# Linear attention followed by a noisy top-2 mixture of experts: queries turned and loaded ahead of keys, key decay on POOL, masks on SyncE's queue

## The chip, the cores and the metric

The kernel runs on one core of a Trainium2 chip. The core has five engines that run side by side and wait for each other through semaphores: TensorE (PE in the profile; its weight loads are PEld), VectorE (DVE), ScalarE (ACT), GpSimd (POOL) and SyncE (SP, which here only issues DMAs). The metric is device microseconds of one execution.

## The reference

Attention with decay over 4 batches, 8 heads, 768 positions and 64 channels, in blocks of 64, and then a mixture of 8 experts on its 3072 rows, each row going to its two best experts.

```
rel = pos[:, None] - pos[None, :]
Dmask = where(rel >= 0, lam ** rel, 0)            # one per head
lam_pow = lam ** (pos + 1);  rev_pow = lam ** (block - 1 - pos)
for b in range(nb):
    intra = (qb @ kb.T * Dmask) @ vb
    inter = (qb * lam_pow) @ kv_state
    out[:, :, sl] = intra + inter
    kv_state = lam ** block * kv_state + (kb * rev_pow).T @ vb
x = out, one row of 512 per token
noisy = x @ w_gate + log1p(exp(x @ w_noise)) * noise
top2 of noisy, weights by softmax of the two
out[token] = sum over its two experts e of weight * (relu(x @ w1[e]) @ w2[e])
```

## The kernel before

**Stages.** The attention works on blocks of 128 positions, two at a time: NST = 12 stages of 256 positions, three to a batch (w = u % 3). Loop number t of the main loop (line 956) finishes stage t and prepares stage u = t + 1. On PE it issues, in this order: the gate products of stage t - 1 (`products`), the turning of its output (`turn_x`), the transposes of keys and queries of stage u (`trans_k`, `trans_q`), the products of keys and values for the state (`kv`), the two halves of the output of stage t (`intra`, `inter`), the logits, and the scores of stage u (`scores`). Each engine takes its instructions strictly in the order in which this program issues them.

**Buffers in PSUM.** `bank()` gives out four buffers named pS in turn. A stage takes eleven: two for `turn_x`, two for the first of the two transposes, two for the other, one for `kv`, four for `scores`. So each waits until the one that was given out four places earlier has been read: the buffer of `kv` is the one that held the first half of the transposes issued first (before: the keys, copied out by four ACT copies on line 331).

**Who reads what.** The transposed keys go to SBUF by ACT in eight copies of 64 partitions (kT), the transposed queries by ACT in two (qT). DVE multiplies the same query buffer with the query scales QS (qTs, line 349), masks the scores (at, line 375) and does the routing work, which the loop hands out in small pieces through `advance(...)`: between the parts of `kv`, behind the logits, and 18 to 24 pieces behind the masking. These pieces exist from t = 4 on. POOL multiplies the states, issues the stores of x and the scattered writes of token lists (lst), and splits weights into high and low parts from t = 5 on (w1l, w2l, line 794).

**Key decay.** `kdecay(u)` (line 351) multiplies keys by the decay factors into KD, which `kv(u)` reads. KD has one buffer. POOL does stages 0 and 1, DVE the ten others.

**Start.** A table of powers of lam is built on DVE, turned by PE, written to DRAM (powd, issued on ACT's queue) and read back twice into the mask tile mrev, named at in the profile, since it takes a buffer of at (lines 227 to 229, ACT's queue). `make_mask` copies it to Mk. QS is a product of four matmuls (line 225) with hsel, which lies in KD's buffer, and pw. SyncE's queue loads lam, then kt, qt, vt of stage 0, then those of stage 1. `keep_warm` issues idle bf16 matmuls.

**Tail.** Behind the loop (lines 1011 to 1019) come the last gate products and logits, the transposes of the first two tiles of expert 0 (`trans_rows`), and its first matmuls. From there the experts run one after the other, from line 1037 on.

Of the kernel before, what the change touches and what calls it, by code (L numbers as in the profile page):

```python
# [21 lines left out]
FT = mybir.dt.float32  # L22
# [4 lines left out]
AF = mybir.ActivationFunctionType  # L27
# [3 lines left out]
B, H, S, D = 4, 8, 768, 64  # L31
C = 128
NC = S // C
NCH = B * NC
HP = H // 2
# [19 lines left out]
NST = NCH // 2  # L55
# [8 lines left out]
ZEROS = {11: 8}  # L64
MID = 16
X1 = ((), (), (), (), (0, 1), (2, 3, 4), (5, 6))
WARM = (10, 1, 1)
GB = (0, 8, 16, NCH)
NG = len(GB) - 1
GM = max(GB[i + 1] - GB[i] for i in range(NG))  # L70
# [17 lines left out]
def sub(ap, offset, dims):  # L88
    return bass.AP(tensor=ap.tensor, offset=ap.offset + offset, ap=dims)
# [27 lines left out]
def kernel(  # L117
# [3 lines left out]
    nc = tc.nc  # L121
# [4 lines left out]
    psum = ctx.enter_context(tc.tile_pool(name="psum", bufs=1, space=bass.MemoryType.PSUM))  # L126
# [9 lines left out]
    powd = dram.tile([256, H], FT, name="powd")  # L136
# [5 lines left out]
    QT, KT, VT = {}, {}, {}  # L142

    def load(u, nm):

        if u >= NST:
            return
        b, w = divmod(u, NW)
        at = b * H * S * D + w * 2 * C * D
        store, src, n = {"qt": (QT, q, 2), "kt": (KT, k, 2), "vt": (VT, v, 3)}[nm]  # L150
        if nm == "qt":
            store[u] = aw.tile([128, 2, H, D], FT, name=nm, bufs=n)
            for a in range(2):
                nc.sync.dma_start(store[u][:, a], sub(src, at + a * C * D, [[D, 128], [S * D, H], [1, D]]))
            return
        store[u] = aw.tile([128, H, 2, D], FT, name=nm, bufs=n)
        step = H if u else H // 2
        for h in range(0, H, step):
            nc.sync.dma_start(store[u][:, h:h + step].rearrange("p h e d -> p h (e d)"),
                              sub(src, at + h * S * D, [[2 * D, 128], [S * D, step], [1, 2 * D]]))  # L160
# [24 lines left out]
    hsel = aw.tile([128, H, 2, D], FT, name="kd", bufs=1).rearrange("p h e d -> p (h e d)")[:H, :HP * C]  # L185
    hsel = hsel.rearrange("h (p s i) -> h p s i", s=2, i=64)
    nc.vector.tensor_copy(hsel, identf[:H, :H].rearrange("h (p s) -> h p s", s=2)[:, :, :, None].to_broadcast([H, HP, 2, 64]))
    pp2 = aw.tile([128, 2 * DB * C], FT, name="xo", bufs=1)[:H, :512].rearrange("p (a i) -> p a i", a=2)
    pw = pp2[:, 0, :]
    nc.vector.memset(pw[:, 128:129], 1.0)  # L190
    nc.vector.tensor_copy(pw[:, 127:128], lamc)
    for i in range(7):
        n = 1 << i
# [5 lines left out]
    p = psum.tile([128, 3, H], FT, name="pL")  # L199
# [5 lines left out]
    mrev = aw.tile([128, C, H], FT, name="at")  # L205
    load(0, "vt")
    Mk = [ac.tile([128, HP, 1 + C], FT, name=f"Mk{s}") for s in range(2)]
    kdc = ac.tile([128, H, 2], FT, name="kdc")
# [11 lines left out]
        return sub(m, 2 * r * (1 + C), [m.ap[0], [1 + C, 2], [1, 2], [1, C]])  # L220

    QS = ac.tile([128, HP, C], FT, name="QS")
    p = psum.tile([128, HP, C], FT, name="pL")
    for hp in range(HP):
        nc.tensor.matmul(p[:, hp, :], hsel[:, hp].rearrange("h s i -> h (s i)"), pw[:, 127::-1], start=True, stop=True)
    nc.scalar.activation(QS, p, AF.Copy)
    for a in range(2):
        nc.scalar.dma_start(mrev[a * 64:(a + 1) * 64].rearrange("p i h -> p (i h)"),
                            sub(powd, 0, [[2 * H, 64], [1, C * H]]))

    for nm in ("kt", "qt", "vt"):
        load(1, nm)
# [87 lines left out]
    def trans_k(u):  # L320

        kT[u] = [aw.tile([128, HP, C], FT, name=f"kT{x}", bufs=1) for x in range(2)]
        for r in range(2):
            p = bank()
            for h in range(4):
                nc.tensor.transpose(p[:, h, :], KT[u][:, 4 * r + h].rearrange("p e d -> p (e d)"), identf)
            for x in range(2):
                for s in range(2):
                    out, src = kT[u][x][half(s), 2 * r:2 * r + 2, :], p[half(s ^ x), s::2, :]
                    if u or x:  # L330
                        nc.scalar.activation(out, src, AF.Copy)  # L331
                    else:
                        nc.vector.tensor_copy(out, src)

    def trans_q(u, scaled=True):

        qT[u] = aw.tile([128, HP, 2 * C], FT, name="qT", bufs=1)
        qTs[u] = aw.tile([128, HP, 2 * C], FT, name="qTs")
        for a in range(2):
            p = bank()  # L340
            for hp in range(HP):
                nc.tensor.transpose(p[:, hp, :], QT[u][:, a, 2 * hp:2 * hp + 2, :], identf)
            cs = slice(a * C, (a + 1) * C)
            if u:
                nc.scalar.activation(qT[u][:, :, cs], p, AF.Copy)
            else:
                nc.vector.tensor_copy(qT[u][:, :, cs], p)
            if scaled and (u % NW or a):
                nc.vector.tensor_mul(qTs[u][:, :, cs], p, QS)

    def kdecay(u):
        if u >= NST:
            return
        KD[u] = aw.tile([128, H, 2, D], FT, name="kd", bufs=1)
        n, eng = (H // 2, nc.gpsimd) if u < 2 else (H, nc.vector)
        for h in range(0, H, n):
            eng.tensor_mul(KD[u][:, h:h + n], KT[u][:, h:h + n], kdc[:, h:h + n, :, None].to_broadcast([128, n, 2, D]))

    TURNS = ((0, 0), (1, 1), (0, 1), (1, 0))

# [69 lines left out]
    def products(u):  # L430

        p = psum.tile([128, 2, C], FT, name="pR")
        for d in range(DB):
            nc.tensor.matmul(p[d * 32:(d + 1) * 32], wgn[:, d, :], XO[u][:, :, d, :], start=True, stop=True)  # L434
        XP[u] = aw.tile([128, 2, C], FT, name="xp", bufs=1)
        nc.scalar.activation(XP[u], p, AF.Copy)
# [20 lines left out]
    def logits(u):  # L457
        nonlocal pl
        if not u:
            pl = psum.tile([128, 512], FT, name="pL")  # L460
            for b in range(NG):
                PC[b] = pl[:, 256 + b % 2 * 128:]
        p = pl[:, :256].rearrange("p (a x) -> p a x", a=2)
        for a in range(2):
            nc.tensor.transpose(p[:, a, :], XP[u][:, a, :], identf)
        b = max(i for i in range(NG) if GB[i] <= 2 * u)
        if 2 * u == GB[b]:
            LG[b] = rp.tile([128, GM, 2 * E], FT, name="l2", bufs=2)
        nc.vector.tensor_reduce(LG[b][:, 2 * u - GB[b]:2 * u - GB[b] + 2, :], p.rearrange("p a (d e) -> p a e d", d=DB)[:, :, :2 * E, :],
                                axis=AX.X, op=ADD)  # L470
# [182 lines left out]
    load_wgn(2)  # L653
    trans_k(0)
    trans_q(0, False)
    nc.vector.tensor_mul(qTs[0][:, :, C:], qT[0][:, :, C:], QS)
    keep_warm(WARM[1])
    kv(0)
# [178 lines left out]
    def trans_rows(t, n):  # L837

        p = psum.tile([128, DB, n], FT, name="pS", bufs=4)
        for d in range(DB):  # L840
            nc.tensor.transpose(p[:, d, :], XG[t][:n, d * 128:(d + 1) * 128], identf[:n, :n])
        hi, lo = [xt(i, slice(t * TS, t * TS + n)) for i in range(2)]
        nc.scalar.activation(hi, p, AF.Copy)  # L843
        nc.vector.tensor_tensor(lo, p, hi.bitcast(FT), op=SUB)  # L844
# [111 lines left out]
    for t in range(NST):  # L956
        u = t + 1
        if t:
            products(t - 1)
            turn_x(t - 1)  # L960
            if t == 8:
                split_low(1, 0, 3, low=nc.gpsimd)
        if u < NST:
            trans_k(u)
        load(t + 3, "kt")
        if u < NST:
            trans_q(u)
        load(t + 3, "qt")
        if u < NST:
            kv(u)  # L970
        if t:
            store_x(t - 1)
            paced(1, XC[t - 1][:, 1, 0, :])
        if u == NST:
            scatter(1)
        if u == NST:
            logits(t - 1)
        intra(t)
        load(t + 3, "vt")
        inter(t, 0)  # L980
        evac_o(t)
        paced(1, XO[t][:, 1, 0, :])
        if t and u < NST:
            logits(t - 1)
        if 2 * t in GB[1:]:
            if 2 * t > GB[1]:
                finish(GB.index(2 * t) - 2, False)
            jobs.append(routing(GB.index(2 * t) - 1))
        advance(FILLB)
        if u < NST:  # L990
            scores(u)
            inter(u, 1)
        kdecay(t + 2)
        for which, j in HIGH.get(t, []):
            split_high(which, 0, j)
        if u < NST:
            if LOW.get(t):
                nc.gpsimd.tensor_copy(spacer, AT[u][0][0:1, 0, 0, 0, 0:1])
            for which, j in LOW.get(t, []):
                split_low(which, 0, j, low=nc.gpsimd)  # L1000
            paced(1, AT[u][1][:, 1, 0, 0, :])
        advance(FILLA.get(t, 18))
        for which, j in LOADS.get(t, []):
            load_w(which, 0, j)
        zero_out(ZEROS.get(t, 0))
        if t == 2:
            turn_noise()
        if t == 4:
            for i in range(4):
                nc.sync.dma_start(sub(lst, i * 128 * LI * RW, [[LI * RW, 128], [1, LI * RW]]), linit)  # L1010
    products(NST - 1)
    for j in range(2):
        trans_rows(j, TS)
    logits(NST - 1)
    head = [mm1(0, 0, PARTS0[0], 0)]
    turn_x(NST - 1)
# [256 lines left out]
```

## Time and profile before

| what | us |
|---|---|
| median of 3 runs (lowest, highest) | 745.12 (744.01, 745.99) |
| the profiled execution: time | 745.11 |
| its span, first to last instruction | 743.3 |
| busy in the span: PE | 706.1 |
| DVE | 371.6 |
| POOL | 293.1 |
| ACT | 239.3 |

The profiled execution is within 0.01 us of the median. 1.8 us of it lie outside the span. Busy times are sums over a long program: what counts for an edit is the stage where it stands, and whether TensorE waits there.

### The profile page before, as it was taken

The numbers are of one execution on the slowest core, as the hardware profiler recorded it, in microseconds if no ns is written. First come the engines' busy times: TensorE is split into PE (matmuls) and PEld (weight loads), VectorE is DVE, ScalarE is ACT, GpSimd is POOL, SyncE is SP. The second block draws the span as 40 slices with busy tenths as digits, with TensorE's granted clock in tenths as the row PEclk, the third lists the DMA queues.
The fourth block names the chain that finished last, engine by engine and source line by source line (L and its number), as shares of the span: only waits on it lengthen the run. The fifth ranks groups of instructions, "written<-read, shape, count | busy, mean of one in ns | idle before, by whom it ended". The sixth has DMA issues, their size and how long they took to land.

```text
span 743.3 us, 15598 instructions
## 1 busy us (share of the span) xinstructions
PE 706.1 (95%) x5975; PEld 600.9 (81%) x5975; DVE 371.6 (50%) x823; ACT 239.3 (32%) x442; POOL 293.1 (39%) x456
## 2 busy tenths in 40 slices
PE   7779888879999999999999999999999999999996
PEld 5667777669988898898889887988798898889885
DVE  4444796977723656555336443644353544335211
ACT  2455665543213333142214221423042322224200
POOL 6211045668885544623152415233412433221311
PEclk9899999999999999999999999999999999999999
DMA  9777867568343766946464636565555656450210
GB/s 204 174 193 208 223 203 191 168 186 246 93 115 101 249 177 175 274 139 195 135 228 133 193 111 231 151 186 176 176 154 173 201 166 193 139 170 14 78 44 36
DMA packets 112754, 122.62 MB, mean 165 GB/s; under 512 B 38155, under 2 KB 81547, under 8 KB 112677
## 3 DMA queue, kind: packets, MB, share of 16 engines
q1 hardware_dynamic: 97732, 80.49, 39.1%
q0 software_dynamic: 14512, 40.57, 17.0%
q8 instruction: 48, 0.79, 0.5%
q10 hardware_dynamic: 432, 0.53, 0.4%
q14 instruction: 30, 0.24, 0.1%
HBM read 87.15 MB, written 35.55 MB: 165 GB/s over the span
## 4 chain that ended last, share of the span: by engine, by line
PE 83%; issue 7%; ACT 3%; DVE 3%; DMA 2%; POOL 1%; SPq 1%; POOLq 0%; DVEq 0%; ACTq 0%
PE pS L879 37%; PE pKV L917 16%; PE pO L917 16%; PE pS L372 3%; PE pO L384 2%; ACT kT L331 2%; PE pO L922 1%; PE pKV L384 1%; PE pS L418 1%; DMA at<-powd 1%; ACT xc L447 1%; PE pS L446 1%; PE pKV L922 1%; PE pR L434 1%; POOL out_dram L936 1%
## 5 line engine op out<-in xcount | busy, mean ns | idle before, releaser
L879 PE MATMUL pS<-xth,w1h 128*128 128x512 f32 (+3 forms) x544 | 181.0, 333 | 0.5 <-ACT xth L843 0.5
L879 PE MATMUL pS<-xtl,w1h 128*128 128x512 f32 (+3 forms) x544 | 180.6, 332 | 0.5 <-DVE xtl L844 0.5
L879 PE MATMUL pS<-xth,w1l 128*128 128x512 f32 (+3 forms) x544 | 180.5, 332 | 0.0
L885 ACT ACTIVATE ht<-pS 128x512 fp32r<-128x512 f32 (+3 forms) x136 | 65.8, 484 | 222.9 <-PE pS L879 220.2
L889 DVE SCALAR_TENSOR_TENSOR ht<-pS,ht 128x256 fp32r<-128x256 f32 (+3 forms) x176 | 76.5, 454 | 111.5 <-ACT ht L885 109.5
L917 PE MATMUL pKV<-w2h,ht 128*128 128x512 f32 x384 | 124.6, 395 | 0.0
L917 PE MATMUL pO<-w2h,ht 128*128 128x512 f32 x384 | 124.3, 394 | 0.0
L936 POOL DMA_INDIRECT out_dram<-ot,rec x46 | 61.3, 1332 | 125.9 <-DVE ot L929 111.6
L879 PEld LDWEIGHTS pS<-xth,w1h 128*128 128x128 f32 x544 | 102.6, 189 | 9.9 <-ACT xth L843 0.8
L879 PEld LDWEIGHTS pS<-xtl,w1h 128*128 128x128 f32 x544 | 102.7, 189 | 9.6 <-DVE xtl L844 0.7
L879 PEld LDWEIGHTS pS<-xth,w1l 128*128 128x128 f32 x544 | 102.6, 189 | 8.8
L917 PEld LDWEIGHTS pO<-w2h,ht 128*128 128x128 f32 x384 | 72.3, 188 | 16.8
L917 PEld LDWEIGHTS pKV<-w2h,ht 128*128 128x128 f32 x384 | 72.3, 188 | 16.8
L917 PE MATMUL pKV<-w2l,ht 128*128 128x512 f32 x192 | 75.8, 395 | 0.0
L917 PE MATMUL pO<-w2l,ht 128*128 128x512 f32 x192 | 75.7, 394 | 0.0
L832 POOL DMA_INDIRECT xg<-x_tok,rec x46 | 51.1, 1111 | 57.5 <-DMA rec<-lst 43.6
L901 POOL DMA_INDIRECT pv<-out_dram,rec x46 | 47.3, 1028 | 28.7 <-issue 28.7
L641 POOL DMA_INDIRECT lst<-recs,dest x48 | 50.3, 1049 | 10.2 <-issue 8.6
L1187 POOL COPY spacer<-ht 1x1 f32<-1x1 f32 x53 | 9.4, 177 | 107.4 <-ACT ht L885 107.4
L929 DVE SCALAR_TENSOR_TENSOR ot<-pKV,rec,pv 128x512 f32<-128x512 f32 x21 | 15.8, 751 | 66.9 <-PE pKV L917 58.4
L929 DVE SCALAR_TENSOR_TENSOR ot<-pO,rec,pv 128x512 f32<-128x512 f32 x21 | 15.8, 750 | 65.0 <-PE pO L917 62.6
L865 ACT ACTIVATE xth<-xg 128x512 fp32r<-128x512 f32 (+1 forms) x39 | 22.4, 598 | 70.2 <-DMA xg<-turned 70.2
(231 smaller groups left out, 1010.0 us busy)
## 6 DMA issues: line engine op xcount, KB each, us to landing
wst<-in_moe_w_dram SPq DMA_DIRECT2D x48, 512.0 KB, 4.4
turned<-ot SPq DMA_DIRECT2D x36, 256.0 KB, 2.9
xg<-turned SPq DMA_DIRECT2D x144, 64.0 KB, 2.0
wst<-in_moe_w_dram SPq DMA_DIRECT2D x32, 256.0 KB, 3.9
qt<-in_q_dram SPq DMA_DIRECT2D x24, 256.0 KB, 6.7
kt<-in_k_dram SPq DMA_DIRECT2D x11, 512.0 KB, 4.8
vt<-in_v_dram SPq DMA_DIRECT2D x11, 512.0 KB, 6.6
x_tok<-xc POOLq DMA_DIRECT2D x8, 512.0 KB, 6.4
```

The costliest lines, as they stand in the source:

```text
L372: nc.tensor.matmul(ps[s][half(a), h, 1 - e, :], keys[:, half(a)], qT[u][half(s), hp, a * C:(a + 1) * C], start=True, stop=True)
L384: nc.tensor.matmul(PO[u][a][half(g), hp, :], lhs, rhs, start=n == 1, stop=n == (12 if u % NW or a else 8))
L641: st = nc.gpsimd.indirect_dma_start(out=lst, out_offset=bass.IndirectOffsetOnAxis(ap=r["dest"][:, i, c:c + 1], axis=0), in_=r["rec"][:, c, ...
L832: nc.gpsimd.indirect_dma_start(out=XG[t][:size(e, t)], out_offset=None, in_=x_tok[:rows, :], in_offset=bass.IndirectOffsetOnAxis(ap=at, ax ...
L865: nc.scalar.activation(hi, p, AF.Copy)
L879: nc.tensor.matmul(p, W1[a][d][:, fs], xt(b, cs)[:, d], start=(d == 0 and i == 0), stop=(d == DB - 1 and i == 2))
L885: nc.scalar.activation(ht(e, 0, f, cs), p, AF.Relu)
L889: nc.vector.scalar_tensor_tensor(ht(e, 1, f, c), p[:, r], 0.0, ht(e, 0, f, c).bitcast(FT), op0=OP.max, op1=SUB)
L901: nc.gpsimd.indirect_dma_start(out=PV[t][:size(e, t), :], out_offset=None, in_=out, in_offset=bass.IndirectOffsetOnAxis(ap=REC[e, t][:, 0: ...
L917: nc.tensor.matmul(p, ht(e, a, f, cs), W2[b][f // 2][:, f % 2, :], start=(i == 0), stop=(i == len(terms) - 1))
L929: nc.vector.scalar_tensor_tensor(o, p, w, pv, op0=MULT, op1=ADD)
L936: st = nc.gpsimd.indirect_dma_start(out=out, out_offset=bass.IndirectOffsetOnAxis(ap=REC[e, t][:, 0:1], axis=0), in_=o, in_offset=None, bo ...
```

## The change

Six edits:

- The QS product (four matmuls, one ACT copy) moves from in front of the first transposes to behind them, and from PSUM buffer pL to pO.
- The two mask reads move from ACT's queue to SyncE's, where they stand behind the loads of stage 0 and ahead of those of stage 1.
- WARM[1] goes from 1 to 5: five idle matmuls in front of `kv(0)`.
- `kdecay` runs on POOL in all stages, in one instruction from stage 2 on.
- In the main loop `trans_q` and the load of qt stand ahead of `trans_k` and the load of kt.
- Behind the loop `trans_rows` of two tiles stands ahead of the last `products`.

```diff
-WARM = (10, 1, 1)
+WARM = (10, 5, 1)
...
     QS = ac.tile([128, HP, C], FT, name="QS")
-    p = psum.tile([128, HP, C], FT, name="pL")
-    for hp in range(HP):
-        nc.tensor.matmul(p[:, hp, :], hsel[:, hp].rearrange("h s i -> h (s i)"), pw[:, 127::-1], start=True, stop=True)
-    nc.scalar.activation(QS, p, AF.Copy)
     for a in range(2):
-        nc.scalar.dma_start(mrev[a * 64:(a + 1) * 64].rearrange("p i h -> p (i h)"),
-                            sub(powd, 0, [[2 * H, 64], [1, C * H]]))
+        nc.sync.dma_start(mrev[a * 64:(a + 1) * 64].rearrange("p i h -> p (i h)"),
+                          sub(powd, 0, [[2 * H, 64], [1, C * H]]))
...
-        n, eng = (H // 2, nc.gpsimd) if u < 2 else (H, nc.vector)
+        n = H // 2 if u < 2 else H
         for h in range(0, H, n):
-            eng.tensor_mul(KD[u][:, h:h + n], KT[u][:, h:h + n], kdc[:, h:h + n, :, None].to_broadcast([128, n, 2, D]))
+            nc.gpsimd.tensor_mul(KD[u][:, h:h + n], KT[u][:, h:h + n], kdc[:, h:h + n, :, None].to_broadcast([128, n, 2, D]))
...
     trans_k(0)
     trans_q(0, False)
+    p = psum.tile([128, HP, C], FT, name="pO")
+    for hp in range(HP):
+        nc.tensor.matmul(p[:, hp, :], hsel[:, hp].rearrange("h s i -> h (s i)"), pw[:, 127::-1], start=True, stop=True)
+    nc.scalar.activation(QS, p, AF.Copy)
     nc.vector.tensor_mul(qTs[0][:, :, C:], qT[0][:, :, C:], QS)
     keep_warm(WARM[1])
...
         if u < NST:
+            trans_q(u)
+        load(t + 3, "qt")
+        if u < NST:
             trans_k(u)
         load(t + 3, "kt")
-        if u < NST:
-            trans_q(u)
-        load(t + 3, "qt")
...
-    products(NST - 1)
     for j in range(2):
         trans_rows(j, TS)
+    products(NST - 1)
     logits(NST - 1)
```

PE at the program's start, before (-) and now (+). pL<-xo,kd and pO<-xo,kd are the QS product, pS<-identf,kt and pS<-identf,qt the transposes of stage 0, pR<-qTs an idle matmul:

```order
 L202 MATMUL pL<-identf,xo 128x8 x2
-L225 MATMUL pL<-xo,kd 128x128 x4
-L326 MATMUL pS<-identf,kt 128x128 x8
-L342 MATMUL pS<-identf,qt 128x128 x8
+L322 MATMUL pS<-identf,kt 128x128 x8
+L338 MATMUL pS<-identf,qt 128x128 x8
+L654 MATMUL pO<-xo,kd 128x128 x4
 L172 LDWEIGHTS qTs
 L172 MATMUL pR<-qTs 128x384
```

The four matmuls of QS have moved behind sixteen transposes. Since they read KD's buffer, the key decay of stage 0 now waits for them there.

SyncE's queue from the loads of stage 0 on, before; kt, qt and vt are the loads of keys, queries and values, wst here the noise:

```order
L159 DMA vt<-in_v_dram 128x4x128 x2
L159 DMA kt<-in_k_dram 128x8x128
L154 DMA qt<-in_q_dram 128x8x64 x2
L159 DMA vt<-in_v_dram 128x8x128
L245 DMA wst<-in_moe_noise_dram 24x1024
L159 DMA kt<-in_k_dram 128x8x128
```

The same place of that queue now, where at<-powd are the two mask reads:

```order
L159 DMA vt<-in_v_dram 128x4x128 x2
L224 DMA at<-powd 64x1024 x2
L159 DMA kt<-in_k_dram 128x8x128
L154 DMA qt<-in_q_dram 128x8x64 x2
L159 DMA vt<-in_v_dram 128x8x128
L241 DMA wst<-in_moe_noise_dram 24x1024
L159 DMA kt<-in_k_dram 128x8x128
```

The reads stand ahead of all loads of stage 1, and these loads now stand behind the wait of the reads for powd.

POOL in loop number 8, now, where kd<-kt,kdc is the key decay of stage 10, lst<-recs,dest a scattered list write and the copies to spacer waits for other engines:

```order
L421 TENSOR_TENSOR S_160<-S_159,QS 128x256
L421 TENSOR_TENSOR S_161<-S_160,QS 128x256
L689 COPY spacer<-xc 1x1
L636 MEMSET spacer 1x1
L637 DMA lst<-recs,dest 29696x2
L689 COPY spacer<-xo 1x1
L636 MEMSET spacer 1x1
L637 DMA lst<-recs,dest 29696x2
L353 TENSOR_TENSOR kd<-kt,kdc 128x1024
L689 COPY spacer<-at 1x1
```

The row of kd is new on POOL; the others stood there before in the same order. On DVE the row of kd behind the four rows of masking is gone in ten loops.

## Rows read from the trace of the kernel before

**Rows 1.** Busy time by engine in two stretches; x counts instructions, PEclk granted clock.
```profile
0.00:165.70 165.70, 134.73 (x2992) 114.14 (x2992) 107.64 (x301) 86.31 (x187) 62.54 (x108) 0.96 0.75 193
165.70:743.30 577.60, 571.32 (x2983) 486.80 (x2983) 263.95 (x523) 152.94 (x255) 230.59 (x348) 1.00 0.52 157
```

**Rows 2.** Waits from 20 to 160 us: total, times, longest.
```profile
PE pS L372 <- issue: 6.5, 5, 2.4
...
PE pS L418 <- ACT kT L331: 4.2, 10, 0.4
...
PE pS L326 <- DVE at L375: 3.7, 1, 3.7
...
PE pL L465 <- DVE pos L585: 2.3, 1, 2.3
...
PE pL L602 <- DVE l L469: 1.6, 1, 1.6
```

**Rows 3.** Timeline, PE, 0 to 14 us: start, us, what, idle before and releaser.
```profile
1.16 3.38 PE L172 MATMUL pR<-qTs 128*128 128x384 bf16 x10 [1.16 <-DVE qTs L166]
...
6.34 2.07 PE L225 MATMUL pL<-xo,kd 8*128 8x128 f32 x8 [1.05 <-ACT kdc L209]
8.34 1.97 PE L326 MATMUL pS<-identf,kt 128*128 128x128 f32 x8
10.10 1.91 PE L342 MATMUL pS<-identf,qt 128*128 128x128 f32 x8
```

**Rows 4.** Timeline of all engines, 0 to 60 us.
```profile
8.56 2.04 POOL L357 TENSOR_TENSOR kd<-kt,kdc 128x512 f32<-128x512 f32 x2 [3.81 <-PE pL L225]
...
9.22 3.12 ACTq L228 DMA_DIRECT2D at<-powd  x2
```

**Rows 5.** Tile powd: the two mask reads from issue to landing.
```profile
DMA to landing us min/median/max: 6.0/7.2/8.5
```

**Rows 6.** Timeline, DVE, 13.9 to 34 us.
```profile
20.48 0.79 DVE L214 COPY Mk<-at 128x512 f32<-128x512 f32 x1 [4.78 <-DMA at<-powd]
21.37 2.48 DVE L375 TENSOR_TENSOR at<-pS,Mk 128x512 f32<-128x512 f32 x4
```

**Rows 7.** Timeline, PE, 13.9 to 34 us.
```profile
16.01 1.98 PE L372 MATMUL pS<-qT,kT 64*64 64x128 f32 x64
...
22.12 1.97 PE L326 MATMUL pS<-identf,kt 128*128 128x128 f32 x8 [3.70 <-DVE at L375]
...
31.56 1.42 PE L372 MATMUL pS<-qT,kT 64*64 64x128 f32 x42 [1.23 <-issue]
```

**Rows 8.** Busy time, 22 to 24 us; columns as in rows 1.
```profile
22.00:24.00 2.00, 1.88 (x9) 1.88 (x10) 1.86 (x4) 0.72 (x2) 0.00 (x0) 0.50 0.68 151
```

**Rows 9.** Timeline, loop number 1, 31 to 47 us, engine by engine.
```profile
34.95 1.04 PE L326 MATMUL pS<-identf,kt 128*128 128x128 f32 x8
...
37.28 1.08 PE L418 MATMUL pS<-vt,kd 64*64 64x64 f32 x29 [0.42 <-ACT kT L331]
...
35.69 3.13 ACT L331 ACTIVATE kT<-pS 64x256 f32<-64x256 f32 x8
38.84 1.09 ACT L345 ACTIVATE qT<-pS 128x512 f32<-128x512 f32 x2
...
39.47 1.29 DVE L349 TENSOR_TENSOR qTs<-pS,QS 128x512 f32<-128x512 f32 x2 [3.61 <-ACT qT L345]
```

**Rows 10.** Tile kd, its row for DVE: ns min/median/max, first and last start.
```profile
L357 DVE TENSOR_TENSOR kd<-kt,kdc x10: 1214/1217/2530, 34.6 to 144.5; 128x1024 f32<-128x1024 f32 x10
```

**Rows 11.** Timeline, DVE and then POOL, 93 to 120 us.
```profile
94.53 2.53 DVE L357 TENSOR_TENSOR kd<-kt,kdc 128x1024 f32<-128x1024 f32 x1
...
93.04 2.35 POOL L794 TENSOR_TENSOR w1l<-wst,w1h 128x1024 fp32r<-128x1024 f32 x1
```

**Rows 12.** Timeline, PE, 148 to 167 us.
```profile
162.47 0.64 PE L434 MATMUL pR<-xo,wgn 128*32 128x256 f32 x8 [1.25 <-ACT xo L405]
...
165.70 0.38 PE L879 MATMUL pS<-xtl,w1h 128*128 128x256 f32 x1 [0.45 <-DVE xtl L844]
```

## The prediction

> **What bounds the kernel now.** I read the busy times by stretch first [rows 1]. Up to 165.7 us, where the experts begin, TensorE (PE) is idle for 165.7 - 134.7 = 31 us; in the 577.6 us behind it, for 6.3 us. The change touches only the first stretch, so PE's idle time and slow clock there are all that it can win. Next come the waits of 20 to 160 us [rows 2]: one long wait of the transposes of stage 1 for the masking on DVE, ten waits of 0.42 us of `kv` for the ACT copies of the keys, two single waits for DVE's routing work, and 6.5 us on the scores alone (some more on other lines) in which PE waits for nothing that the profile names. Then the start, engine by engine. The reader is to see one chain there: the mask reads land, DVE copies the mask at 20.48, masks from 21.37 [rows 6], and the transposes of stage 1, which need a score buffer, start at 22.12 after 3.70 us of idle PE [rows 7].
>
> **The start.** Before, the QS product (2.07 us) stands in front of the key transposes, which start when it ends, at 8.34 [rows 3]. Now they can start at 6.3 or a little earlier, the queries behind them at about 8.2, if these have landed; the trace shows them landed by 10.10. The QS product then runs from about 10.1 to 12.2. KD's buffer holds hsel, so the key decay of stage 0 on POOL, 8.56 before, starts only then; its two halves take 2.04 us [rows 4], so `kv(0)` can start at 13.2 on its first half, against 12.3 before. Five idle matmuls fill that second: ten took 3.38 us [rows 3], so the four new ones cost 1.35 us, of which at most 0.4 lie outside the wait. I put the scores of stage 0 at 16.5 (bounds: 16.0 as before, and 18.1 if the queries come at 10.1), against 16.01 [rows 7].
>
> The mask reads were issued on ACT from 9.22 on [rows 4], behind the QS copy and beside the loads of stage 1, and took 6.0 and 8.5 us to land [rows 5]. On SyncE they wait for powd alone, which had landed by 9.22, and stand ahead of the loads of stage 1. By the shorter time they land at 15.2, by the longer one with half a us for the second issue at 18.2, against 20.4; I take 16. The mask copy (0.79) then ends at about 17, the first scores are there at 17.5, and the first masking (a quarter of 2.48, 0.62) frees its buffer at 18.1 instead of 22.0. PE has the other output work of stage 0 until then, so the transposes of stage 1 start at about 19.1 instead of 22.12: 3.0 us. SyncE holds the loads of stage 1 behind the reads for some 3 us; issued from about 10 on, and landing no later after their issue than the slower mask read [rows 5], they are there at about 19, when the first of them is needed; I cost that at nothing, and up to 1 us if the values of stage 1 come late.
>
> The clock comes on top. In the 3.70 us of idle PE the granted clock fell, and it is 0.50 of full, the 1.2 GHz level, from 22 to 24 us [rows 8]; eight transposes took 1.97 us there and 1.04 at the 2.4 GHz level [rows 7, 9]. With no idle stretch in front, sixteen transposes and the products behind them would save some 2.4 us. I count 1.4 of it, since the next thing on PE is an unnamed wait that ended at 31.56 [rows 7], and part of what comes sooner only waits longer there. The start: -3.0 - 1.4 = -4.4 us, bounds -1.9 (mask at 18.2, its copy done at 19.0, transposes at 20.2, the clock no better) and -5.4 (all of the 2.4).
>
> **The loop.** Of the eleven loops that prepare a stage, number 0 is counted above. In the ten others `kv` gets the buffer of the first half of what is transposed first. Before: four of eight key copies (half of 3.13 us) behind the copies of x, and PE waits 0.42 us for them [rows 9], 4.2 us in ten [rows 2]. Now: one query copy (half of 1.09) and, where the stage is not first in its batch, one DVE product (half of 1.29) [rows 9]. ACT's sum is unchanged, and the scores, which need all copies, come 3 us later, so the swap costs nothing there. Where DVE is free, 0.25 to 0.42 us go in each of six loops: 2.0. In the loops with routing pieces DVE's product stands behind 18 to 24 of these, so `kv` may now wait for DVE: the new wait. It has behind it on PE everything of that stage. I set those four at nothing for `kv`.
>
> Key decay on DVE took 1.22 us in most loops and at worst 2.53 [rows 10], some 14 us in ten; on POOL I estimate 2.05 each from the two halves [rows 4]. On POOL it stands behind the state products and in front of the waits for the masking, where POOL idles; `kv` needs it a whole loop later. DVE idles in the early loops, so its gain counts only where PE waits for DVE: 1.6 us at the routing product and 2.3 at the last logits [rows 2]. The second chain also starts with the query product, which now comes ahead of the eight key copies, so up to 3.13 us earlier [rows 9]. I take 0.7 and 1.2 of them. Sum 2.0 + 1.9 = 3.9, of which the unnamed waits behind take 0.9: -3.0 us. Bounds: -5.2 (all ten kv waits or nearly, and more of the 3.9 at DVE), and +2, if `kv` waits 1 us for DVE in each of four loops and nothing else comes.
>
> As to these unnamed waits: one stands in most loops, up to 2.4 us long, always in a run of short matmuls [rows 2, 7]. The Trainium skill ("Runtime: NRT & Kernel Launch", Instruction fetch mechanics) says that engines stream instructions in 16 KiB blocks and that crossing a block is mostly hidden. By that the 0.9 would be 0 and the sum 0.9 us lower. The trace does not show this stretch hidden, if that is what it is; no row here proves it.
>
> **The tail.** The last gate products wait 1.25 us for ACT's copies of the output; the first expert matmul that needs all inputs starts at 165.70 [rows 12]. The transposes of two gathered tiles need nothing of that and move into the wait. ACT then does the copies of the tiles first. I take -1.2, bounds 0 (ACT's own queue sets it) and -1.3.
>
> **Sum.** -4.4 - 3.0 - 1.2 = -8.6. From the profiled execution's own time (745.11, which is the median but for 0.01): 736.5 us. With all terms at their better bounds 733.2, at their worse 745.2.
>
> **The rivals.** (A) The start and the tail come, the loop gives nothing: what `kv` gains is lost to the unnamed waits and to the new wait for DVE. For it: such a wait stands behind `kv` in most loops; against it: they were not in front of the two DVE waits. 745.1 - 4.4 - 1.2 = 739.5.
>
> (B) The start hardly moves: powd's landing and the query load set it, not the order of instructions. For it: the DMA engines are three quarters busy over this stretch [rows 1]; against it: the reads are now in front of 1.5 MB of loads. -1.9 at the start, -1.2 at the tail, half of the loop: 740.5; nothing in the loop: 742.
>
> (C) Slower: POOL's key decay holds DVE up. DVE's decay took 2.53 us instead of 1.22 where it overlapped a 2.35 us subtraction on POOL that began 1.5 us before it [rows 10, 11]: it ended 1.7 us after POOL's did. So a DVE instruction that reads two SBUF tiles stood still while POOL read. The routing pieces are mostly such instructions, and each hold-up of 2.05 us stands in front of the query product, for which `kv` now waits. Place: loops 4 to 9. It decides if POOL comes to the decay only when DVE has begun its pieces; in loops 8 and 9 it comes behind list writes, so late. Against it: in the other loops it comes while DVE masks, which reads PSUM. Six hold-ups cost 12.3, less the 5.6 of start and tail: 751.8; four of them 747.7, which I take.
> The Trainium skill ("SBUF — State Buffer", Who interferes with whom) makes this a rule: a DVE instruction with two SBUF inputs contends with a GpSimd instruction that reads SBUF, and one blocks until the other is done. By that rule the time is that of (C) wherever the two meet; the two rows agree with it.
>
> (D) No change: the experts' first gathers wait for list writes on POOL, which the ten decays push back, and what comes early is given back at 185 to 210 us: 745.
>
> **How the numbers follow.** Forecast 0.50, its own range 733.2 to 739; A 0.20; B 0.12; C 0.10; D 0.08. About 0.3% (2.2 us) is what a measurement of this kernel can tell from no change, so faster means under 742.9 and slower over 747.4. Faster: all of the forecast, nearly all of A, two thirds of B, a tenth of D: 0.78. Slower: most of C and the worse half of a late start with waits in the loop: 0.08. Same: 0.14. The range reaches from the better bounds, a little beyond (732.5), over A and B to 743.5; it leaves out C, D and the ends.
>
> **What would show it.** Right: the first mask copy on DVE at about 16 to 17 us, the first transposes of stage 1 at about 19, with a granted clock of 1.00 there; `kv` without a wait for ACT in loops 1 to 4; the last logits' wait for DVE halved; PE idle up to the experts' first matmul 23 to 25 us instead of 31. Wrong: the mask copy still at 20; `kv` waiting for DVE's query product for more than 1 us in loops 6 to 10; routing instructions of over 1 us next to POOL's decay; new PE idle time behind the experts' start.

## The result and the profile after

The changed kernel takes 735.89 us (median of 4 runs, 734.95 to 736.56), the kernel before 744.57 beside it (4 runs, 741.76 to 745.99): ratio 0.9887, 95% interval 0.9855 to 0.992. The profiled execution of the changed kernel took 736.56 us, with a span of 734.8.

The first view is again the busy time in two stretches, cut where the experts' first matmul with all its inputs begins: 157.12 us now, 165.70 before [rows 1]. Columns as in rows 1.

```profile
0.00:157.12 157.12, 132.89 (x2997) 111.78 (x2997) 100.36 (x291) 84.63 (x187) 77.21 (x116) 0.97 0.77 201
157.12:734.76 577.64, 571.24 (x2983) 486.72 (x2983) 263.98 (x523) 152.65 (x255) 228.98 (x351) 1.00 0.52 158
```

All of the gain lies ahead of that point: 8.58 us. Behind it the program takes 577.64 us against 577.60. PE's idle time in the first stretch fell from 31.0 to 157.12 - 132.89 = 24.2 us.

Next the waits of PE from 20 to 160 us (total, times, longest), to be held against rows 2.

```profile
PE pS L368 <- issue: 8.2, 7, 2.5
PE pS L414 <- issue: 5.6, 7, 1.8
PE pL L598 <- DVE l L465: 1.9, 1, 1.9
PE pL L461 <- DVE pos L581: 1.7, 1, 1.7
```

L414 is `kv`. It waits 5.6 us now, more than the 4.2 us of before [rows 2], only in fewer and longer waits; the label "issue" hides what it waits for. The routing product (L598) waits longer than before, the last logits (L461) shorter. So the loops did not win where the forecast had put it.

The start of the changed kernel, from the timelines of SyncE's queue, PE and DVE:

```profile
9.70 1.15 SPq L224 DMA_DIRECT2D at<-powd  x2
...
15.21 0.32 PE L172 MATMUL pR<-qTs 128*128 128x384 bf16 x1 [1.75 <-DVE S L422]
15.46 3.43 PE L368 MATMUL pS<-qT,kT 64*64 64x128 f32 x64
18.65 0.89 PE L380 MATMUL pKV<-qTs,S 64*64 64x128 f32 x8
19.47 0.66 PE L338 MATMUL pS<-identf,qt 128*128 128x128 f32 x4
20.44 0.63 PE L338 MATMUL pS<-identf,qt 128*128 128x128 f32 x4 [0.32 <-DMA qt<-in_q_dram]
...
15.07 0.64 DVE L214 COPY Mk<-at 128x512 f32<-128x512 f32 x1
```

The tile's own view has the landing of the two mask reads:

```profile
DMA to landing us min/median/max: 4.0/4.2/4.3
```

The reads leave at 9.70 instead of 9.22 and land after 4.0 and 4.3 us, not 6.0 and 8.5 [rows 5]. DVE copies the mask at 15.07 instead of 20.48 [rows 6], and the transposes of stage 1 start at 19.47 instead of 22.12 [rows 7]. But the scores of stage 0 (15.46) now take 3.43 us, where they took 1.98. The busy time around them shows why (PEclk is the third column from the right); first the changed kernel, then the kernel before:

```profile
14.00:16.00 2.00, 0.79 (x17) 0.54 (x20) 0.98 (x2) 1.16 (x1) 0.62 (x1) 0.95 1.22 273
16.00:18.00 2.00, 2.00 (x44) 2.00 (x40) 0.79 (x2) 0.00 (x0) 1.44 (x2) 0.50 1.39 203
18.00:20.00 2.00, 2.00 (x31) 1.71 (x24) 1.58 (x3) 0.00 (x0) 2.00 (x4) 0.70 1.14 291
20.00:22.00 2.00, 1.63 (x14) 1.29 (x12) 1.16 (x3) 1.47 (x4) 2.00 (x6) 1.00 1.01 251
```

```profile
16.00:18.00 2.00, 2.00 (x69) 1.99 (x70) 0.00 (x0) 0.00 (x0) 2.00 (x4) 1.00 1.17 206
18.00:20.00 2.00, 0.42 (x8) 0.17 (x4) 0.00 (x0) 0.00 (x0) 2.00 (x6) 1.00 1.10 215
```

The granted clock is 1.00 from 20 us on, where it was 0.50 before [rows 8]; but it now falls to 0.50, the 1.2 GHz level, already at 16 to 18 us, behind the gaps that PE has from 11 to 15 us. The slow stretch moved forward, and from 20 us on it is gone.

Last the tail, on PE, against rows 12:

```profile
153.99 1.09 PE L841 MATMUL pS<-identf,xg 128*128 128x128 f32 x8
155.31 0.64 PE L430 MATMUL pR<-xo,wgn 128*32 128x256 f32 x8 [0.23 <-ACT xo L401]
156.56 0.44 PE L461 MATMUL pL<-identf,xp 128*128 128x128 f32 x2 [0.62 <-ACT xp L432]
```

The wait of 1.25 us is 0.23 now; 0.62 of it came back as a wait of the last logits.

### The profile page after: what moved, and what is told of

It reads as the page before. It is cut to its first block, busy times and chain, and to the rows that moved or that the text cites. A ratio compares the mean times of both kernels' runs of the same rounds, so it can differ in the third digit from the quotient of the medians.

```text
span 734.8 us, 15624 instructions
## 1 busy us (share of the span) xinstructions
PE 704.1 (96%) x5979; PEld 598.5 (81%) x5979; DVE 364.3 (50%) x813; ACT 237.3 (32%) x442; POOL 306.2 (42%) x466
## 4 chain that ended last, share of the span: by engine, by line
PE 85%; issue 7%; DVE 3%; DMA 2%; POOL 2%; SPq 1%; ACT 1%; POOLq 0%; ACTq 0%; DVEq 0%
PE pS L879 37%; PE pKV L917 16%; PE pO L917 16%; PE pS L368 3%; PE pO L380 2%; PE pO L922 2%; PE pKV L380 1%; PE pS L442 1%; PE pS L414 1%; DMA vt<-in_v_dram 1%; PE pKV L922 1%; PE pS L322 1%; PE pS L338 1%; POOL out_dram L936 1%; PE pR L430 1%
```

## The experiments

Twelve runs of kernels, in three groups that ran together. One execution says little of a stretch: the same code for the start gave 31.8 to 34.0 us in four kernels. So this table puts all executions side by side. "Start" is the first `turn_x` on PE, "loops" from there to the eleventh, "tail" from there to the experts' first matmul with all inputs; the next two are PE's waits in the loops (0.15 us and more): at `kv`, and at other places without a named cause. e7 is left out: its profiled execution took 756.0 us, 8 above its median.

| kernel | start | loops | tail | at kv | unnamed |
|---|---|---|---|---|---|
| before | 34.02 | 120.98 | 10.70 | 4.2 | 11.6 |
| e4, tail only | 31.92 | 120.20 | 8.64 | 3.4 | 10.9 |
| e1, start only | 29.45 | 117.83 | 12.94 | 4.2 | 10.4 |
| e2, swap only | 32.73 | 119.69 | 10.06 | 6.2 | 9.7 |
| e3, decay only | 31.81 | 125.01 | 11.87 | 5.1 | 12.8 |
| changed | 29.71 | 118.76 | 8.65 | 5.6 | 8.1 |
| e5, changed again | 29.16 | 116.44 | 11.17 | 6.2 | 6.4 |
| e12, mask reads on ACT | 29.92 | 117.57 | 8.37 | 4.5 | 10.3 |
| e8, swap undone | 28.89 | 118.70 | 11.62 | 4.6 | 8.0 |
| e6, decay on DVE | 29.23 | 117.10 | 11.19 | 7.9 | 5.1 |
| e10, the same again | 29.23 | 115.75 | 8.64 | 4.9 | 7.5 |
| e9, queries first to loop 5, decay on DVE | 29.06 | 115.38 | 10.50 | 2.8 | 8.6 |
| e11, the same, decay on POOL | 29.85 | 119.85 | 10.89 | 2.9 | 10.3 |

**Each part alone.** Four kernels, beside runs of the kernel before (744.5 us, 29 runs). e1 has the edits to the start:

```diff
-WARM = (10, 1, 1)
+WARM = (10, 5, 1)
...
-        nc.scalar.dma_start(mrev[...
+        nc.sync.dma_start(mrev[...
...
     trans_q(0, False)
+    (the QS product stands here)
```

> The kernel before with the edits to the start alone (QS product behind the first transposes, mask reads on SyncE's queue, five idle matmuls). Theory (the start gives 4.3 us by itself, and the loops hand it through): turn_x of stage 0 on PE at 29.7, the experts' first matmul at 161.4, time 740.4. Rival (the early start came from the swap of queries and keys or the key decay too, since the loads of stage 1 are late): turn_x of stage 0 at 31 to 33, time 742 to 744.

Measured: 740.49 us, ratio 0.9949 (0.9924 to 0.9973), so -3.8 us (-5.7 to -2.0); start at 29.45. The theory holds.

```diff
         if u < NST:
+            trans_q(u)
+        load(t + 3, "qt")
+        if u < NST:
             trans_k(u)
         load(t + 3, "kt")
-        if u < NST:
-            trans_q(u)
-        load(t + 3, "qt")
```

> The kernel before with queries ahead of keys in the loops and nothing else. Theory (the swap gives what loops 1 to 6 gained, about 6 us, and brings the loss in the later loops only together with the key decay on POOL): loops 1 to 6 shorter by 4 to 6 us in all, loops 7 and 9 not longer; time 739 to 741. Rival (the unnamed waits give little back without the decay moved off DVE, and kv waits for DVE's query product in loops 6 to 10): under 2 us in loops 1 to 6, loops 7 and 9 longer by over 1 us each; time 744 to 746.

Measured: 742.06 us, ratio 0.9948 (0.9926 to 0.9971), -3.9 us (-5.5 to -2.2). That is a gain, 742.06 lying 1.1 us above the theory's times and 1.9 below the rival's. But its profiled execution (743.09, above its median) shows loops of 119.69, and `kv` waits 6.2 us in it, 1.4 each in loops 6, 7 and 9, and 1.0 in loop 10. The gain in time is shown, its place isn't.

```diff
-        n, eng = (H // 2, nc.gpsimd) if u < 2 else (H, nc.vector)
+        n = H // 2 if u < 2 else H
...
-            eng.tensor_mul(KD[u][...
+            nc.gpsimd.tensor_mul(KD[u][...
```

> The kernel before with the key decay of all stages on POOL and nothing else. Theory (POOL's decay holds DVE up where the two meet, and takes some load off DVE otherwise): loops 1 to 5 within 1 us of before in all, some later loop longer by 1 to 2 us with a DVE instruction of over 1 us beside a POOL decay; time 744 to 748. Rival (taking the decay off DVE is what gained in the loops): loops 1 to 6 shorter by 3 us or more; time 739 to 742.

Measured: 749.1 us, ratio 1.0073 (1.0043 to 1.0103), +5.4 us (+3.2 to +7.7): a loss, and a little more than the theory had. Loop 6 took 16.83 us in the profile (12.21 before), and its largest wait is an unnamed one on PE, in the middle of the output products:

```profile
100.12 0.37 PE L384 MATMUL pKV<-at,vt 64*64 64x128 f32 x1 [3.63 <-issue]
```

Behind it the clock falls, so that the next 3.9 us run at half speed:

```profile
96.20:100.10 3.90, 0.29 (x11) 0.05 (x3) 3.22 (x6) 1.07 (x2) 1.57 (x3) 0.84 0.97 201
100.10:104.00 3.90, 3.88 (x51) 3.24 (x50) 2.19 (x3) 1.07 (x2) 1.66 (x1) 0.50 0.40 149
```

DVE was held up there as well (four routing pieces took 3.65 us beside POOL's decay), but no record joins this to PE's wait, of which more stands under the unnamed waits below. That the decay on POOL costs is shown by the times; that this wait is the reason in most executions is not.

```diff
-    products(NST - 1)
     for j in range(2):
         trans_rows(j, TS)
+    products(NST - 1)
```

> The kernel before with the transposes of two gathered tiles ahead of the last gate products and nothing else. Theory: loop 11 (last turn_x to the experts' first matmul) 10.70 before, now 9.0 to 9.5, time 743.5. Rival (the 2.05 us that the tail gave came mostly from the earlier decay and routing pieces, not from the order): loop 11 at 10.4 or more, time 744.5 or more.

Measured: 744.39 us, ratio 1.0 (0.9975 to 1.0025). The tail took 8.64 us in the profiled execution, even less than the theory's 9.0 to 9.5, but that was the fastest of ten runs, and the table has 8.4 to 11.6 for this order and 10.1 to 12.9 for the other. The means (9.96 of nine, 11.39 of four) differ by 1.4 us, which the times neither show nor exclude: theory and rival stay undecided.

**Decay and swap in the changed kernel.** In this group the kernel before took 755.94 us (21 runs), 11 us more than in the others. In all four kernels profiled here the longer part is the one behind the experts' start, which no edit touches: it takes 585 to 590 us, and PE waits 4.6 to 7.7 us in it, against at most 1.4 in the other groups. In e5:

```profile
156.77:742.60 585.83, 573.00 (x2983) 486.89 (x2983) 263.89 (x523) 152.43 (x255) 230.78 (x351) 1.00 0.50 154
```

So only ratios to the kernel before beside it are used. e5 is the changed kernel itself.

> The changed kernel again, unchanged, beside the three below on one chip. Expected by all theories: 736 to 737. Its profile is a second execution: what holds in both (loops 7 and 9 longer than before by over 1 us) belongs to the change, what differs by more than 1 us (the landing of the mask reads, the unnamed waits) doesn't.

Measured: ratio 0.9907 (0.9859 to 0.9954), in us 749.74. Loop 7 took 15.23 us again (15.22 in the first execution, 13.80 before); loop 9 took 12.47 (14.90 in the first, 12.61 before): its unnamed wait of 2.54 us was 1.06, and the clock, at 0.50 for 3.4 us behind that wait in the first execution, did not fall. So the loss in loop 9 does not belong to the change. That in loop 7 came in both executions, but e12 below, whose loops have the same code, took 12.64 us there: the change can bring it and need not.

```diff
-        n = H // 2 if u < 2 else H
+        n, eng = (H // 2, nc.gpsimd) if u < 2 else (H, nc.vector)
...
-            nc.gpsimd.tensor_mul(KD[u][...
+            eng.tensor_mul(KD[u][...
```

> The changed kernel with the key decay of stages 2 to 11 back on DVE. Theory (POOL's decay holds DVE's routing pieces up, and that costs more than DVE saves): loops 7 and 9 back to 12 to 13.5 us each, loops 1 to 6 as in the changed kernel within 1 us in all, no DVE instruction of 3.65 us; time 733 to 735, which is under the changed kernel's. Rival (the swap needs the decay off DVE, since kv now waits for DVE's query product): kv waits for DVE 1 us or more in several of loops 5 to 10, time 738 to 741.

Measured: ratio 0.9854 (0.9817 to 0.989), 744.6 us, the best of the group; its interval and e5's overlap. Loop 7 took 12.31 us. Part of the rival is there too: in loop 10 `kv` waits for DVE's query product, which stands behind routing pieces and comes at 135.74.

```profile
136.47 0.37 PE L414 MATMUL pS<-vt,kd 64*64 64x64 f32 x2 [2.86 <-DVE qTs L345]
```

```diff
-        n = H // 2 if u < 2 else H
+        n, eng = (H // 2 if u < 2 else H), (nc.vector if u >= 8 else nc.gpsimd)
...
-            nc.gpsimd.tensor_mul(KD[u][...
+            eng.tensor_mul(KD[u][...
```

> The changed kernel with the key decay on POOL for stages up to 7 (issued in loops up to 5 or 6) and on DVE for stages 8 to 11. Theory (it costs only where it meets routing pieces): loops 1 to 5 as in the changed kernel, loops 7 and 9 as in e6, time within 1 us of e6. Rival (the loss of loops 7 and 9 comes from kv behind DVE's query product, whoever does the decay): loops 7 and 9 at 14 to 15 as in the changed kernel, time 736 to 737.

Measured: ratio 0.9889 (0.9835 to 0.9944), 748.32 us: too wide to place between e5 and e6. It tells nothing.

```diff
         if u < NST:
+            trans_k(u)
+        load(t + 3, "kt")
+        if u < NST:
             trans_q(u)
         load(t + 3, "qt")
-        if u < NST:
-            trans_k(u)
-        load(t + 3, "kt")
```

> The changed kernel with keys ahead of queries again in the loops. Theory (the swap carries the gain of loops 1 to 6 and also keeps DVE's hold-up off the products with the states, as the query product is done before POOL's decay begins): kv waits 0.4 us each for ACT's key copies again, loop 6 or 7 holds a wait of 2 us or more on the products with the states; time 743 to 746. Rival (additive parts: swap worth 3.9 us): time 740.

Measured: ratio 0.9963 (0.9927 to 0.9998), 752.36 us, against 0.9907 with the swap: by the medians the swap is worth 0.0056, some 4.2 us, in the changed kernel as by itself, with intervals that overlap. The rival's size fits. The theory's waits of 2 us on the state products did not come; the longest named wait in the loops is 2.10 us, of the routing product for DVE.

**Can it be better, and what the mask queue gives.** The third group stands beside 744.8 us of the kernel before (11 runs).

```diff
-        if u < NST:
-            trans_q(u)
-        load(t + 3, "qt")
-        if u < NST:
-            trans_k(u)
-        load(t + 3, "kt")
+        pair = [(trans_q, "qt"), (trans_k, "kt")]
+        for trans_any, nm in pair if u < 7 else pair[::-1]:
+            if u < NST:
+                trans_any(u)
+            load(t + 3, nm)
```

> The changed kernel with the key decay of stages 2 to 11 on DVE and queries ahead of keys in loops 0 to 5 only (keys first from loop 6 on). Theory (queries first wins 0.2 us a loop where DVE is free, and loses where kv then waits for DVE's query product or for the first key bank: 1.4, 1.4, 1.6 and 2.9 us in loops 6, 7, 9 and 10 of e6): kv waits 0.4 to 0.5 in loops 6 to 10, loops 6 to 10 shorter than e6's by 3 to 5 us in all, time 2 to 4 us under e6's. Rival (what waits at kv would otherwise wait at the unnamed places or at DVE's logits): loops 6 to 10 within 1.5 us of e6's, time within 1.5 us.

Measured: 736.91 us, ratio 0.9903 (0.9871 to 0.9935). `kv` waits 2.8 us in all instead of 4.9 or 7.9, as expected, and the time is no better than e6 and e10: the rival. What is saved at `kv` in these loops is lost at other places: the unnamed waits sum to 8.6 us here and to 5.1 and 7.5 there, and loop 7 has 1.78 us at the routing product here and 1.38 in e10.

> The kernel of e6 again, on one chip with the two beside it. Theory (decay on POOL costs some 4 us net): ratio to before 0.985 to 0.988, under the changed kernel's 0.9887 and 0.9907. Rival (e6 was a lucky draw): 0.989 to 0.991.

Measured: 735.33 us, ratio 0.9878 (0.9852 to 0.9903). The fastest kernel in this group. The ratio lies where the theory had it, but its interval reaches into the rival's, and it lies within that of the changed kernel. Its loops took 115.75 us.

> The changed kernel (decay on POOL) with queries ahead of keys in loops 0 to 5 only. Theory (both edits have a part in the loss of loops 7 and 9: kv behind the query product by the swap, DVE held up by the decay): a hold-up of DVE of over 1 us stays, loops 6 to 10 between those of e9 and of the changed kernel, time 3 to 5 us over e9. Rival (all of the loss comes from the swap in these loops): time within 1 us of e9.

Measured: 738.68 us, ratio 0.9911 (0.9884 to 0.9938); loop 7 at 16.22 us against 14.13 in e9, with a wait of 2.10 at the routing product. In time it is 1.8 us behind e9, with intervals that overlap, which is neither the theory's 3 to 5 us nor the rival's 1. Loops 6 to 10 sum to 65.1 us, above e9 (61.6) and the changed kernel (63.8), and not between them. For the fourth time the kernel with the decay on POOL is the slower one (e3, e5 against e6, e11 against e9, and the changed kernel against e10).

```diff
-        nc.sync.dma_start(mrev[...
+        nc.scalar.dma_start(mrev[...
```

> The changed kernel with the mask reads on ACT's queue again, behind the QS copy, and all else as changed. Theory (the queue of the mask reads gives most of the start): mask reads issued at 11 instead of 9.7 and landing beside the loads of stage 1, mask copy on DVE at 19 to 21 instead of 15.1, turn_x of stage 0 at 31 to 32.5 instead of 29.2 to 29.7, time 2 to 3 us over the changed kernel's. Rival (the transposes ahead of the QS product and the idle matmuls give it): turn_x of stage 0 under 30.2, time within 1 us.

Measured: 736.79 us, ratio 0.9889 (0.9862 to 0.9916), the same as the changed kernel's 0.9887; start at 29.92. The rival holds. But the edit does not put the reads back behind the QS copy, as the expectation says: the copy (12.68) now comes behind them. The rows of e12, ACT's queue, DVE and PE:

```profile
9.85 1.14 ACTq L224 DMA_DIRECT2D at<-powd  x2
...
17.61 0.64 DVE L214 COPY Mk<-at 128x512 f32<-128x512 f32 x1 [2.06 <-DMA at<-powd]
...
16.01 3.26 PE L368 MATMUL pS<-qT,kT 64*64 64x128 f32 x64
19.11 0.60 PE L380 MATMUL pKV<-qTs,S 64*64 64x128 f32 x8
19.64 1.09 PE L338 MATMUL pS<-identf,qt 128*128 128x128 f32 x8
```

The mask comes 2.5 us later than with the reads on SyncE, and the transposes of stage 1 only 0.17 us later. With the slow scores and the state products ahead of them, PE is not ready before 19.5 in the changed kernel and 19.7 in e12.

## Why the prediction was right in time, and where its steps failed

The forecast was 736.5 and the time 735.89. Term by term, with the profiled pair first and then the means over the executions in the table that share the code of that stretch:

**The start: forecast -4.4; -4.31 in the pair, -3.3 in the mean** (32.6 of four executions to 29.3 of eight), and -3.8 in time (e1). The size is right, half of its mechanism is not. The mask copy at 15.07 and the transposes at 19.47 came about where the working had them. But the working let the masking set the transposes. In the changed kernel the scores of stage 0, at the 1.2 GHz level, set them, and e12 shows that the queue of the reads, by itself, gives nothing that can be measured. The two edits that are left of the start (the QS product behind the first transposes, the idle matmuls) were not tried apart, so which of them carries the 3.3 us stays open.

That the mask comes at 17.6 in e12 and not at 19 to 20.5, with the reads on the same queue as before, has a cause in the trace that the working did not have: it took the two reads to leave half a us apart. Before, ACT's queue takes 3.12 us for them [rows 4]: the second leaves at 11.88, when the load of the keys of stage 1, which counts up the same semaphore, has landed (11.86; in e4 11.46 and 11.44). In e12 and in the changed kernel it shares its semaphore with a load of stage 0 and leaves 0.54 and 0.57 us behind the first. In e12 the second read lands 2.9 us sooner than before: half of that is its earlier issue (10.39), the other half its shorter time to land, 7.1 us instead of 8.5.

The clock term came, but not alone. From the transposes of stage 1 to the first `turn_x` the program takes 10.24 us (29.71 - 19.47) instead of 11.90, so the 1.4 us counted there are there. The fall of the clock, however, moved ahead to the scores of stage 0, which lose 1.45 (3.43 instead of 1.98). Nor does the start hang on that fall. In e11, with the same code, the clock did not fall:

```profile
16.56 1.98 PE L368 MATMUL pS<-qT,kT 64*64 64x128 f32 x64
...
18.90 0.66 PE L338 MATMUL pS<-identf,qt 128*128 128x128 f32 x4
20.68 0.63 PE L338 MATMUL pS<-identf,qt 128*128 128x128 f32 x4 [1.12 <-DMA qt<-in_q_dram]
```

There the scores take 1.98 us and the transposes begin at 18.90, but PE then waits 1.12 us for the queries of stage 1, a load that the forecast had cost at nothing, and the start is at 29.85.

**The loops: forecast -3.0; -2.22 in the pair, -2.1 in the mean** (119.7 of before, e1 and e4; 117.6 of the changed kernel, e5 and e12; the two sets of three overlap). The sum is near, and each of its parts failed, so that it is near is luck. Two of the forecast's own signs of being wrong appeared: `kv` waits 1.8 us for DVE's query product in loop 6, and routing instructions of over 1 us stand beside POOL's decay.

- *"2.0 at `kv`".* `kv` waits more than before, 5.6 to 6.2 us in the two executions of the changed kernel. Loops 1 to 5 went as the working has it: 0.25 us or nothing, instead of 0.42. But in loops 7 and 9 `kv` waits 1.3 to 1.4 us, and not for DVE. The view of e10's loop 7, ACT and DVE and then PE:

```profile
98.54 3.14 ACT L327 ACTIVATE kT<-pS 64x256 f32<-64x256 f32 x8
...
102.75 1.28 DVE L345 TENSOR_TENSOR qTs<-pS,QS 128x512 f32<-128x512 f32 x2
```

```profile
100.14 0.33 PE L414 MATMUL pS<-vt,kd 64*64 64x64 f32 x4 [1.38 <-ACT kT L327]
```

  The first four of the eight key copies end at 98.54 + 3.14 / 2 = 100.11, and `kv` starts there, long before DVE's query product. (In the changed kernel the copies start at 98.97, so that the fourth ends at 100.54; `kv` starts at 100.62, the query product at 103.77.) `kv` reads no transposed keys, so only a buffer ties it to them: there it has that of the first half of the keys, which now come second. The step that failed is the one that took the buffers to be given out strictly in turn. In loop 6 of the changed kernel it does wait for DVE, 1.8 us, as the "new wait" of the working.

- *"0.7 and 1.2 at the two waits for DVE".* The routing product waits 1.90 us now (1.58 before), the last logits 1.74 (2.29), so 0.2 us of the 1.9 came. DVE is held up by the mechanism of rival C. DVE and POOL of the changed kernel in loops 6 and 7:

```profile
90.88 3.65 DVE L110 SCALAR_TENSOR_TENSOR wacc<-wacc,wu 128x8 f32<-128x8 f32 x4
...
102.15 1.70 DVE L583 SCALAR_TENSOR_TENSOR own<-ob,pos 128x8 f32<-128x8 bf16 x1
...
92.38 1.92 POOL L353 TENSOR_TENSOR kd<-kt,kdc 128x1024 f32<-128x1024 f32 x1
...
101.92 1.89 POOL L353 TENSOR_TENSOR kd<-kt,kdc 128x1024 f32<-128x1024 f32 x1 [2.06 <-issue]
```

  And the same two rows of e10, where DVE does the decay:

```profile
92.50 1.21 DVE L110 SCALAR_TENSOR_TENSOR wacc<-wacc,wu 128x8 f32<-128x8 f32 x4
...
102.66 0.17 DVE L583 SCALAR_TENSOR_TENSOR own<-ob,pos 128x8 f32<-128x8 bf16 x1
```

  Four pieces that take 1.21 us take 3.65, of which the third 2.60, and one that takes 0.17 takes 1.70. The two held up end at 94.33 and 103.84, POOL's decays at 94.30 and 103.81. The routing product, 1.90 us late (1.38 in e10), waits behind the second. This repeats to within 0.05 us in e5. So a DVE instruction with two inputs stood still while POOL read two. The Trainium skill ("SBUF — State Buffer", Who interferes with whom) states this as a rule, and here the trace agrees. Rival C had the mechanism and the loops, and too high a price: a hold-up of over 1 us comes in two loops (6 and 7; in e12 also in 9) and not in four to six, and in e12 the routing product does not wait at all. The cost of the decay in time is 5.4 us alone, and by ratios 4.0 (e5 against e6), 0.7 (changed against e10) and 0.6 (e11 against e9) in the changed kernel, the last three with overlapping intervals.

- *"The unnamed waits take 0.9".* They gave: 10.4 to 11.6 us in the three kernels with the loops of before, 6.4 to 10.3 in the three with the loops of the changed kernel. Nothing in the forecast had them shrink, and in these executions this carried the term. They are no fixed cost of a place, since the one in loop 9 was 2.54 and 1.06 us in two executions of one program.

  The records of the DMA packets tell what they are. In the wait of 3.63 us of e3 the queue that carries instructions moves one block:

```profile
q8 instruction: 1, 0.02, 2.1%
```

  This packet of 16,384 bytes runs from 97.26 to 98.52, and PE goes on 1.60 us after its end. In many other waits the packet has ended before PE stands still, so that a view of the wait alone shows none. Over all fourteen profiled executions, from 20 to 150 us, PE has 137 unnamed waits of 0.2 us and more outside `kv`, and 134 of them end 1.2 to 1.7 us after the end of such a packet; of the 150 other waits there, 15 do. The instruction behind such a wait also has the same place in PE's order whatever the kernel, to within one: the 706th, 1218th, 1729th, 2241st and 2753rd record of PE and its weight loads, for example, 511 or 512 apart. So PE waits there for its next block of instructions. By the Trainium skill ("Runtime: NRT & Kernel Launch", Instruction fetch mechanics) the crossing of a block of instructions is mostly hidden; the traces don't agree, with 5 to 13 us in ten loops. No run changes the number of instructions, so what of the time hangs on these waits, and why one is longer than another, is not shown.

**The tail: forecast -1.2; -2.05 in the pair, -1.4 in the mean.** The wait moved as described; the pair's larger figure is the spread of this stretch.

**The rivals.** A had the loops give nothing: in the mean they give 2.1, and its 739.5 is 3.6 us too high. C's 747.7 fell by its price. B fell with the start. D fell with 577.64 against 577.60. The parts alone sum to -3.8 - 3.9 + 5.4 + 0.0 = -2.3 us and together gave -8.4. Most of that gap does not need the swap: e8, which is the start, the decay and the tail with keys first, gave -2.8 (0.9963) where its parts sum to +1.6. So the decay cost less there than alone. Why is not shown; the wait of 3.63 us in loop 6 of e3 has no like in e8. The intervals of the parts allow some of the gap.

## What to carry to other kernels

Where a wait is found, ask what PE would do if it were gone: here the mask could come 2.5 us later without a loss, as the scores ahead of it ended only at 19.3. Be slow to put two-input work on POOL beside DVE's chain of small instructions: what DVE saves in a stretch where nobody waits for it, it loses where PE does. Hold a wait without a named cause against the packets of the queue that carries instructions, also those that end just before it. And take a stretch of a single trace only with a second execution beside it: here the changed kernel's loops and tail each moved by over 2 us from one run to the next, and the unchanged start by as much.

## What the runs showed of the hardware that was not expected

- PE stood still for 5 to 13 us of the loops at the borders of its instruction blocks: 134 of 137 unnamed waits end 1.2 to 1.7 us after the end of a packet of 16,384 bytes on the instruction queue.
- A DVE instruction with one tensor input was held up by POOL's decay as well: TENSOR_SCALAR gn<-ga, 0.19 us beside no decay (before), took 1.62 us in e12 and ended at 125.49, the decay at 125.43.
- The same code for the start took 31.8 to 34.0 us over four executions, with the landing of the mask reads (mask copy at 19.05 to 20.56); with the changed start it stayed within 28.9 to 29.9.
- Moving PE's work closer together did not by itself keep the clock up. In the changed kernel gaps of 0.32, 0.76 and 1.75 us between 11 and 15 us preceded the fall to 0.50 at 16 us, and the clock fell at 14.6 to 16.3 us in eight of the nine kernels of the table with the changed start. The ninth, e11, whose PE was busy until 14 us (its five idle matmuls took 1.78 us, not 0.99), kept 1.00, and the kernel before, busy until 14 us too, kept it through 20 us with a gap of 1.75 us at the same place.
- The kernel before took 11 us more in one group of runs than in the other two; the four kernels profiled in that group took 8 to 13 us more in the experts' part, with the granted clock at 0.99 to 1.00 there.
